# Values ahead of the probability transposes in an attention step: a fused attention and two-layer FFN kernel

## The chip, the cores and the metric

One NeuronCore of a Trainium2 chip runs the whole program. The metric is the device time of one execution in microseconds; three runs of the kernel before gave 641.52, 641.78 and 646.76 us, and their median is 641.78 us.

## The reference, cut to what matters

The inputs are q, k and v of 2 batches, 8 heads, 768 positions and 64 columns, and the weights of two feed-forward layers (512 to 2048 and back), which arrive as 64-bit floats.

```python
scores = q @ k.T / sqrt(64) + bias        # bias: minus a slope of the head times the distance
scores = where(is_global | is_local, scores, -1e9)   # 8 global keys, 96 local keys
a = softmax(scores)                       # exp(scores - max) / (sum + 1e-9)
x = (a @ v).transpose(0, 2, 1, 3).reshape(1536, 512)
x = silu(x @ w_in1) @ w_out1              # layer 1
out = hardswish(x @ w_in2) @ w_out2       # layer 2
```

## The kernel before, in words

**Units and steps.** A unit is a pair of heads and half a sequence (384 queries); there are 16 units of three tiles of 128 queries, so 48 steps in `seq` (line 442). `attention_loop(n)` (line 448) runs several stages of different steps in one turn. Turn n issues, in this order on TensorE:

- `stage_b` (line 379), the **scores** of step n: six matmuls, in pairs. Each contracts over the 64 columns of one head, so the array is used as two tiles of 64 rows (profile form `64*128`). The tile written is psS.
- `stage_c` (line 410), the **transposes of the probabilities** of step n-3 (CL = 3): four (two in a sequence's first tile) 128 by 128 transposes into psT. They use the whole array (`128*128`). The result is copied to the tile pt, by VectorE (line 419), or by ScalarE (line 421) where t is 0.
- `stage_d` (line 424), the **values** of step n-4 (LAG = 4): eight (or four) matmuls into psO, which read the pt that turn n-1 made. Each head's output has 64 columns, so the array is used as two tiles of 64 columns (`128*64`). Where t is 2, the last of a unit, ScalarE copies psO to xh (line 439), and VectorE makes the remainder xl (line 440) a turn later.
- a **piece of the feed-forward** part from `stream`, if turn n has one: 12 matmuls of `h_piece` (psH, line 510) or six of `y_piece` (psY, line 683), whole array. Pieces stand in even turns from 16; the first six places hold two pieces only (turns 16 and 22), and from turn 28 every even turn has one. Beside the turns that have transposes or values there are 14 of them, up to turn 50.
- `transposes(n)` (line 480), since APOS is 2: the **transposes of raw keys** (turns that are 2 modulo 3) or **queries** (turns that are 0 modulo 3) of a later unit into psA, three or four, whole array (lines 331 to 348). Turns that are 1 modulo 3 have none.

Turns 48 to 51 have no scores any more, only the last transposes and values with pieces. After that the program is feed-forward work alone, paced by `when` (line 210).

**Between the stages.** VectorE adds the bias and takes the extremum of the scores (line 394), ScalarE takes the exponential and its sum (line 398), VectorE the reciprocal (lines 404 and 405), GpSimd scales (line 407); then come the transposes. psS has two banks and one shared bank, psT and psA share a ring of three, psO has two.

**What sets the order.** Attention is issued under `manual_schedule` for TensorE, ScalarE and GpSimd (line 799): these run in program order. VectorE's order, and that of the loads on SyncE's queue, comes from the framework's planner, which follows program order among what it takes to be ready. Beside its own part each engine has the decoding of the 64-bit weights (lines 101 to 148), spread over the turns through `slots`.

Of the kernel before, what the change touches and what calls it, by code (L numbers as in the profile page):

```python
# [28 lines left out]
def attention_ffn_kernel(ctx, tc, q, k, v, n_global, n_local, w_in1, w_out1, w_in2, w_out2, out):  # L29
# [32 lines left out]
    def bank(tag, name):  # L62
        return psum.tile([P, 512], F32, name=name, tag=tag, bufs=ps_bufs[tag])
# [133 lines left out]
    CL = 3  # L197
# [44 lines left out]
    def loads_v(u):  # L242
        b, half, p = units[u]
        s0 = half * TB
        rv = apool.tile([P, 2, HB, D], F32, name=f"rv{u}", tag="rv")
        vp = apool.tile([P, 2, HB, D], F32, name=f"vp{u}", tag="vp")
        i0 = 1 - half
        for h in range(2):
            vh = v[b, 2 * p + h]
            nc.sync.dma_start(rv[:, h], vh[s0:s0 + TB].rearrange("(t p) d -> p t d", p=P))  # L250
            f0 = s0 - P + i0 * P
            nc.sync.dma_start(vp[:G0, h, i0:], vh[f0:f0 + (HB - i0) * P].rearrange("(t p) d -> p t d", p=P)[G:])
            nc.sync.dma_start(vp[G0:, h, i0:], vh[:G].unsqueeze(1).to_broadcast([G, HB - i0, D]))
        raw[u][3:] = rv, vp
# [44 lines left out]
    def beyond():  # L299

        fl, ng, nl = small[:, 2:5], nval[:, 0:1], nval[:, 1:2]
        nc.vector.tensor_scalar(out=fl[:, 0:1], in0=nl, scalar1=1.0, scalar2=None, op0=ALU.is_lt)
        nc.vector.tensor_scalar(out=fl[:, 1:2], in0=nl, scalar1=float(NLOC_MAX), scalar2=None, op0=ALU.is_gt)
        nc.vector.tensor_scalar(out=fl[:, 2:3], in0=ng, scalar1=float(NGLOB_MAX), scalar2=None, op0=ALU.is_gt)
        nc.vector.tensor_tensor(out=fl[:, 0:1], in0=fl[:, 0:1], in1=fl[:, 1:2], op=ALU.add)
        nc.vector.tensor_tensor(out=fl[:, 0:1], in0=fl[:, 0:1], in1=fl[:, 2:3], op=ALU.add)
        nc.vector.tensor_copy(flag, fl[:, 0:1])
# [3 lines left out]
    def biases(p):  # L311

        nbs[p] = [cpool.tile([P, 2, w], F32, name=f"{n}{p}", tag=f"{n}{p}") for n, w in (("nbB", P), ("nbA", W))]
        for nb, dist in zip(nbs[p], (distB, distA)):
            for h in range(2):
                nc.gpsimd.tensor_scalar(out=nb[:, h, :], in0=dist, scalar1=slopes[2 * p + h], scalar2=1.0, op0=ALU.mult, op1=ALU.mult)
# [59 lines left out]
    def first(u, t):  # L376
        return units[u][1] == 0 and t == 0

    def stage_b(n, u, t):
        b, half, p = units[u]  # L380
        kh, kl, qh, ql = tr[u]
        tags = ("SS", "fS", "Sf")[n % 3] if n < PRE - 1 else "SS"
        ps = [bank(tags[h], f"psS{u}_{t}_{h}") for h in range(2)]
        o = P if first(u, t) else t * SP
        for i, (a, c) in enumerate(((qh, kh), (qh, kl), (ql, kh))):
            for h in range(2):
                hs = slice(h * D, (h + 1) * D)
                nc.tensor.matmul(ps[h][:, :W], a[hs, t * P:(t + 1) * P], c[hs, o:o + W], start=i == 0, stop=i == 2)
        w, nb = (P, nbs[p][0]) if first(u, t) else (W, nbs[p][1])
        z = apool.tile([P, 2, W], F32, name=f"z{u}_{t}", tag="z", bufs=ZB)  # L390
        mn = apool.tile([P, 2], F32, name=f"mn{u}_{t}", tag="mn", bufs=3)
        sm = apool.tile([P, 2], F32, name=f"sm{u}_{t}", tag="sm", bufs=3)
        for h in range(2):
            nc.vector.tensor_tensor_reduce(  # L394
                out=z[:, h, :w], in0=ps[h][:, :w], in1=nb[:, h, :], scale=1.0, scalar=3e38,
                op0=ALU.add, op1=ALU.min, accum_out=mn[:, h:h + 1])
        for h in range(2):
            nc.scalar.activation(out=z[:, h, :w], in_=z[:, h, :w], func=AF.Exp, bias=mn[:, h:h + 1], scale=-1.0,  # L398
                                 accum_out=sm[:, h:h + 1])
        zt[u, t], smt[u, t] = z, sm  # L400

    def stage_b2(u, t):
        z, sm, w = zt[u, t], smt.pop((u, t)), P if first(u, t) else W
        nc.vector.tensor_scalar(out=sm, in0=sm, scalar1=1e-9, scalar2=None, op0=ALU.add)  # L404
        nc.vector.reciprocal(sm, sm)  # L405
        for h in range(2):
            nc.gpsimd.tensor_scalar(out=z[:, h, :w], in0=z[:, h, :w], scalar1=sm[:, h:h + 1], scalar2=1.0,  # L407
                                    op0=ALU.mult, op1=ALU.mult)

    def stage_c(u, t):  # L410
        z = zt.pop((u, t))
        n = 1 if first(u, t) else 2
        ps = bank("tr", f"psT{u}_{t}").rearrange("p (h c q) -> p h c q", h=2, c=2)
        for h in range(2):
            for c in range(n):
                nc.tensor.transpose(ps[:, h, c, :], z[:, h, c * P:(c + 1) * P], ident)
        pt = apool.tile([P, 2, 2, P], F32, name=f"pt{u}_{t}", tag="pt")
        if t:
            nc.vector.tensor_copy(pt[:, :, :n, :], ps[:, :, :n, :])
        else:  # L420
            nc.scalar.copy(pt[:, :, :n, :], ps[:, :, :n, :])
        ptt[u, t] = pt

    def stage_d(u, t):
        b, half, p = units[u]
        rk, kp, rq, rv, vp = raw[u]
        pt = ptt.pop((u, t))
        if t == 0:
            pso[0] = bank("o", f"psO{u}")
        ps = pso[0]  # L430
        n = 1 if first(u, t) else 2
        for c in range(n):
            for h in range(2):
                lhs = (rv if c == n - 1 else vp)[:, h, t, :]
                nc.tensor.matmul(ps[h * D:(h + 1) * D, t * P:(t + 1) * P], lhs, pt[:, h, c, :], start=c == 0, stop=c == n - 1)
        if t == HB - 1:
            i = 2 * b + half
            hi, lo = (x[:, p, i * TB:(i + 1) * TB] for x in (xh, xl))
            nc.scalar.copy(hi, ps[:, :TB])
            return lambda: nc.vector.tensor_tensor(out=lo, in0=ps[:, :TB], in1=hi.bitcast(F32), op=ALU.subtract)  # L440

    seq = [(u, t) for u in range(len(units)) for t in range(HB)]
    queue, late, rests, now = {}, {}, {}, [0]

    def at(n, f):
        queue.setdefault(n, []).append(f)

    def attention_loop(n):
        for f in queue.pop(n, []):
            f()  # L450
        if n < len(seq):
            u, t = seq[n]
            stage_b(n, u, t)
            if t == HB - 1 and u + 1 < NP:
                biases(u + 1)
        if n == 0:
            e, r = stage_a(1, 0)
            e()
            r()
            beyond()  # L460
        if 0 <= n - 1 < len(seq):
            stage_b2(*seq[n - 1])
        for f in rests.pop(n, []):
            f()
        if APOS == 0:
            transposes(n)
        if 0 <= n - CL < len(seq):
            stage_c(*seq[n - CL])
        if 0 <= n - LAG < len(seq):
            u, t = seq[n - LAG]  # L470
            f = stage_d(u, t)
            if f:
                at(n + 1, f)
                if u + 2 < len(units):
                    loads_v(u + 2)

        if APOS == 1:
            transposes(n)

    def transposes(n):  # L480
        for d, part in ((KOFF, 0), (QOFF, 1)):
            if (n + d) % HB == 0 and 1 <= (n + d) // HB < len(units):
                e, r = stage_a((n + d) // HB, part)
                e()
                rests.setdefault(n + 1, []).append(r)
                if part and (n + d) // HB + 2 < len(units):
                    loads((n + d) // HB + 2)
# [298 lines left out]
    def loop(n):  # L786
        now[0] = n
        attention_loop(n)
        f = todo.get(n)
        if f:  # L790
            f[0](*f[1:])
        if APOS == 2:
            transposes(n)
        for f in late.pop(n, []) + slots.pop(n, []):
            f()
# [269 lines left out]
```

## Time and profile before

| | |
|---|---|
| runs | 641.52, 641.78, 646.76 us; median 641.78 us |
| profiled execution, first to last instruction | 638.6 us |
| granted TensorE clock, mean | 0.999 |
| TensorE busy | 617.2 us, 97% of the span |
| VectorE busy | 489.9 us, 77% |
| ScalarE busy | 417.4 us, 65% |
| GpSimd busy | 161.0 us, 25% |

The profile tells the span of the profiled execution and no other time of it, so 638.6 us is the time against which rows are summed; the median of the runs is 3.2 us above it, for what lies before the first and after the last instruction recorded. A TensorE row gives the modelled end of a matmul, which overlaps the next one's start, so that the time that a group of matmuls takes on the engine is read from its start to the start of the next group, not from its duration.

### The profile page before, as it was taken

How to read it: one execution, taken by the hardware profiler on the slowest of the kernel's cores; microseconds unless marked ns; L12 is line 12 of the kernel's file. 1: busy time of each engine (PE TensorE's matmuls, PEld its weight loads, DVE VectorE, ACT ScalarE, POOL GpSimd, SP SyncE). 2: the span in 40 equal slices, each digit the busy share in tenths (PEclk: the TensorE clock that was granted, in tenths of full speed). 3: DMA queues.
4: the chain of work that ended last, by engine and by line, in shares of the span. 5: the costliest groups of instructions: out<-in, count | busy, mean ns of one | idle time of the engine just before them, and what ended most of it. 6: DMA issues, size and time to landing. Idle time of an engine off the chain costs nothing.

```text
span 638.6 us, 9729 instructions
## 1 busy us (share of the span) xinstructions
PE 617.2 (97%) x3214; PEld 498.9 (78%) x3214; DVE 489.9 (77%) x1107; ACT 417.4 (65%) x887; POOL 161.0 (25%) x233
## 2 busy tenths in 40 slices
PE   5889999999999999999999998999999999999996
PEld 3667777789888788888888887887788888888885
DVE  5899889953578796767675679988979696969453
ACT  4787877765557576666666676765766666666760
POOL 2776666561111111111212120011111111111110
PEclk9999999999999999999999999999999999999999
DMA  6555645349577667777776793186576868686544
GB/s 174 136 139 136 149 112 137 99 150 204 103 162 166 144 146 176 161 180 166 181 163 134 164 198 100 66 247 150 132 173 165 182 157 181 157 176 162 100 102 166
DMA packets 81625, 97.31 MB, mean 152 GB/s; under 512 B 55456, under 2 KB 55456, under 8 KB 81312
## 3 DMA queue, kind: packets, MB, share of 16 engines
q0 software_dynamic: 12576, 45.09, 37.7%
q1 hardware_dynamic: 68992, 51.53, 26.8%
q8 instruction: 27, 0.44, 0.3%
q14 instruction: 30, 0.25, 0.1%
HBM read 46.27 MB, written 3.15 MB: 77 GB/s over the span
## 4 chain that ended last, share of the span: by engine, by line
PE 35%; issue 25%; POOL 5%; DVE 2%; DMA 2%; ACT 1%; POOLq 0%; ACTq 0%; SPq 0%; DVEq 0%
PE psY L683 19%; PE psH L510 9%; POOL y L712 5%; PE psP_b L591 3%; PE psP_c L591 2%; PE psP_a L591 2%; DMA y<-st 1%; DMA raw<-in_moe_w_in_dram 1%; ACT st L708 0%; DVE g L541 0%; DVE da L1027 0%; DVE wol L148 0%; DVE dc L134 0%; DVE u L608 0%; ACT da L103 0%
## 5 line engine op out<-in xcount | busy, mean ns | idle before, releaser
L712 POOL DMA_DIRECT2D y<-st x78 | 66.9, 857 | 362.4 <-ACT st L708 357.2
L708 ACT COPY st<-psY 128x512 f32<-128x512 f32 x156 | 91.3, 586 | 51.6 <-PE psY L683 47.5
L510 PE MATMUL psH<-xh,wih 128*128 128x512 f32 (+1 forms) x216 | 83.2, 385 | 1.7 <-DVE g L541 1.7
L510 PE MATMUL psH<-xl,wih 128*128 128x512 f32 (+1 forms) x216 | 82.5, 382 | 0.0
L510 PE MATMUL psH<-xh,wil 128*128 128x512 f32 (+1 forms) x216 | 82.4, 382 | 0.0
L683 PE MATMUL psY<-gh,woh 128*128 128x512 f32 (+1 forms) x160 | 61.4, 384 | 0.0
L683 PE MATMUL psY<-gh,wol 128*128 128x512 f32 (+1 forms) x160 | 60.6, 378 | 0.0
L683 PE MATMUL psY<-gl,woh 128*128 128x512 f32 (+1 forms) x160 | 60.5, 378 | 0.0
L398 ACT ACTIVATE z<-z,mn 128x256 f32<-128x256 f32 (+1 forms) x96 | 46.5, 486 | 21.1 <-DVE mn L394 15.6
L407 POOL TENSOR_SCALAR z<-z,sm 128x256 f32<-128x256 f32 (+1 forms) x96 | 48.2, 514 | 43.9 <-DVE sm L405 18.4
L683 PE MATMUL psY<-woh,gl 128*128 128x512 f32 x144 | 56.1, 390 | 0.1
L683 PE MATMUL psY<-woh,gh 128*128 128x512 f32 x144 | 56.1, 390 | 0.1
L683 PE MATMUL psY<-wol,gh 128*128 128x512 f32 x144 | 56.0, 389 | 0.0
L510 PEld LDWEIGHTS psH<-xh,wih 128*128 128x128 f32 x216 | 40.5, 188 | 10.6 <-DVE g L541 2.1
L103 ACT ACTIVATE da<-raw 128x512 f32<-128x512 f32 x64 | 42.9, 670 | 5.9 <-DMA raw<-in_moe_w_in_dram 5.5
L510 PEld LDWEIGHTS psH<-xl,wih 128*128 128x128 f32 x216 | 40.5, 188 | 7.5 <-DVE xl L620 0.4
L510 PEld LDWEIGHTS psH<-xh,wil 128*128 128x128 f32 x216 | 40.5, 188 | 7.1
L1027 DVE SCALAR_TENSOR_TENSOR da<-raw,da 128x512 int32<-128x512 int32 x64 | 44.3, 693 | 1.2 <-DVE sm L404 0.2
L608 DVE TENSOR_TENSOR u<-psP_c,u 128x512 f32<-128x512 f32 x22 | 15.1, 688 | 34.5 <-ACT u L602 34.5
L532 ACT ACTIVATE a<-psH 128x512 f32<-128x512 f32 (+1 forms) x24 | 14.2, 590 | 40.4 <-PE psH L510 40.3
L551 DVE SCALAR_TENSOR_TENSOR gl<-a,gh 128x512 fp32r<-128x512 f32 (+1 forms) x34 | 23.2, 682 | 21.9 <-ACT gh L545 21.6
L1015 DVE TENSOR_SCALAR da<-da 128x512 f32<-128x512 f32 x64 | 28.3, 442 | 14.7 <-ACT da L103 14.7
(185 smaller groups left out, 1565.2 us busy)
## 6 DMA issues: line engine op xcount, KB each, us to landing
y<-st POOLq DMA_DIRECT2D x78, 512.0 KB, 4.8
raw<-in_moe_w_in_dram SPq DMA_DIRECT2D x32, 512.0 KB, 4.1
raw<-in_moe_w_out_dram SPq DMA_DIRECT2D x32, 512.0 KB, 3.3
rk<-in_k_dram SPq DMA_DIRECT2D x32, 96.0 KB, 2.5
rq<-in_q_dram SPq DMA_DIRECT2D x32, 96.0 KB, 2.9
rv<-in_v_dram SPq DMA_DIRECT2D x32, 96.0 KB, 2.6
out_dram<-y SPq DMA_DIRECT2D x12, 256.0 KB, 2.0
xf<-xh SPq DMA_DIRECT2D x2, 1024.0 KB, 6.7
```

The lines of the kernel that those rows point to most:

```text
L103: nc.scalar.activation(out=t["a"], in_=raws[n][:, :, 1].bitcast(F32), func=AF.Abs)
L398: nc.scalar.activation(out=z[:, h, :w], in_=z[:, h, :w], func=AF.Exp, bias=mn[:, h:h + 1], scale=-1.0, accum_out=sm[:, h:h + 1])
L407: nc.gpsimd.tensor_scalar(out=z[:, h, :w], in0=z[:, h, :w], scalar1=sm[:, h:h + 1], scalar2=1.0, op0=ALU.mult, op1=ALU.mult)
L510: nc.tensor.matmul(ps, a[:, kt, js], x[:, kt, n0:n1], start=n == 0, stop=n == 3 * KT - 1)
L551: nc.vector.scalar_tensor_tensor(out=gl[:, j, :], in0=t["a"], scalar=2.0, in1=gh[:, j, :].bitcast(F32), op0=ALU.mult, op1=ALU.subtract)
L591: nc.tensor.matmul(ps, a[:, 2 * k + q, f * P:(f + 1) * P], x, start=p in (1, 5) and n == 0, stop=n == 5, skip_group_check=True)
L608: nc.vector.tensor_tensor(out=u, in0=st["c"], in1=u, op=ALU.add)
L683: nc.tensor.matmul(ps[:, :rhs.shape[1]], lhs, rhs, start=n == 0, stop=n == 3 * FC - 1)
L708: nc.scalar.copy(st[:, m % 2, :], part)
L712: late.setdefault(n, []).append(lambda: nc.gpsimd.dma_start(y, st, accum_op=ALU.add))
L1015: nc.vector.tensor_scalar(out=a, in0=a, scalar1=as_float(897 << 20), scalar2=as_float((1151 << 20) - 1), op0=ALU.max, op1=ALU.min)
L1027: nc.vector.scalar_tensor_tensor(out=ai, in0=w1, scalar=-0x40000000, in1=ai, op0=ALU.bitwise_and, op1=ALU.bitwise_or)
```

## The change

In `attention_loop` the call of `stage_d` for step n-4 moves ahead of the call of `stage_c` for step n-3. TensorE's order in a turn becomes scores, values, transposes of the probabilities, piece, raw transposes. Along with `stage_d` move the copy of psO to xh on ScalarE (where t is 2) and the loads of the values of unit u+2, which are issued behind it. In turns that are 0 modulo 3 both `stage_c` (t = 0) and `stage_d` (t = 2) have work on ScalarE, so there the copy to xh now stands ahead of the copy to pt.

```diff
         if APOS == 0:
             transposes(n)
-        if 0 <= n - CL < len(seq):
-            stage_c(*seq[n - CL])
         if 0 <= n - LAG < len(seq):
             u, t = seq[n - LAG]
             f = stage_d(u, t)
@@
                 at(n + 1, f)
                 if u + 2 < len(units):
                     loads_v(u + 2)
+        if 0 <= n - CL < len(seq):
+            stage_c(*seq[n - CL])
```

## Rows read from the trace of the kernel before

**Rows 1.** The page, busy time, share of the span and instructions of each engine

```profile
PE 617.2 (97%) x3214; PEld 498.9 (78%) x3214; DVE 489.9 (77%) x1107; ACT 417.4 (65%) x887; POOL 161.0 (25%) x233
```

**Rows 2.** Windows of 40 us: length, busy us and instructions by engine, clock, DMA

```profile
20.00:60.00 40.00, 35.89 (x324) 25.41 (x323) 37.47 (x142) 31.19 (x104) 29.32 (x49) 1.00 0.62 152
60.00:100.00 40.00, 38.66 (x322) 28.92 (x322) 36.48 (x135) 29.89 (x99) 25.93 (x40) 1.00 0.53 133
100.00:140.00 40.00, 39.85 (x345) 30.52 (x341) 33.33 (x119) 29.04 (x94) 27.09 (x40) 1.00 0.39 97
```

**Rows 3.** Waits of TensorE: us in total, times, longest us

```profile
PE psO L435 <- DVE pt L419: 2.9, 3, 1.1
```

**Rows 4.** Timeline, TensorE, 103 to 108: start us, us, operation, [idle before]

```profile
103.48 0.44 PE L683 MATMUL psY<-gh,woh 128*128 128x384 f32 x1
103.76 0.34 PE L683 MATMUL psY<-gl,woh 128*128 128x384 f32 x1
103.94 0.34 PE L683 MATMUL psY<-gh,wol 128*128 128x384 f32 x1
...
105.60 0.66 PE L416 MATMUL psT<-ident,z 128*128 128x128 f32 x4
106.18 0.44 PE L435 MATMUL psO<-pt,rv 128*64 128x128 f32 x4
106.55 0.39 PE L388 MATMUL psS<-kh,qh 64*128 64x256 f32 x2
...
107.11 0.66 PE L416 MATMUL psT<-ident,z 128*128 128x128 f32 x4
107.70 0.44 PE L435 MATMUL psO<-pt,vp 128*64 128x128 f32 x4
```

**Rows 5.** Timeline, TensorE, 109 to 113

```profile
109.44 0.49 PE L331 MATMUL psA<-ident,rk 128*128 128x128 f32 x3
109.77 0.27 PE L346 MATMUL psA<-ident,kp 128*128 128x128 f32 x1
...
111.70 0.55 PE L331 MATMUL psA<-ident,rq 128*128 128x128 f32 x3
112.17 0.39 PE L388 MATMUL psS<-kh,qh 64*128 64x256 f32 x2
...
112.73 0.66 PE L416 MATMUL psT<-ident,z 128*128 128x128 f32 x4
```

**Rows 6.** Timeline, TensorE's weight loads, 103 to 104

```profile
103.48 0.19 PEld L683 LDWEIGHTS psY<-gh,woh 128*128 128x128 f32 x1 [0.17 <-issue]
103.59 0.19 PEld L683 LDWEIGHTS psY<-gl,woh 128*128 128x128 f32 x1
```

**Rows 7.** Timeline, TensorE, 136 to 138, a turn without scores

```profile
136.54 0.60 PE L416 MATMUL psT<-ident,z 128*128 128x128 f32 x4
137.07 0.44 PE L435 MATMUL psO<-pt,vp 128*64 128x128 f32 x4
...
137.66 0.66 PE L416 MATMUL psT<-ident,z 128*128 128x128 f32 x4
```

**Rows 8.** Timeline, VectorE, the copies at 106.86 and 138.35

```profile
106.86 0.68 DVE L419 COPY pt<-psT 128x512 f32<-128x512 f32 x1
...
138.35 0.69 DVE L419 COPY pt<-psT 128x512 f32<-128x512 f32 x1 [0.48 <-PE psT L416]
```

**Rows 9.** Timeline, ScalarE, 112 to 113

```profile
112.31 0.56 ACT L421 COPY pt<-psT 128x512 f32<-128x512 f32 x1
112.77 0.48 ACT L439 CAST xh<-psO 128x384 fp32r<-128x384 f32 x1
113.14 0.50 ACT L337 ACTIVATE qh<-psA 128x384 fp32r<-128x384 f32 x1
```

**Rows 10.** Timeline, TensorE, 27 to 30, an early turn

```profile
27.89 0.66 PE L416 MATMUL psT<-ident,z 128*128 128x128 f32 x4
29.63 0.51 PE L435 MATMUL psO<-pt,vp 128*64 128x128 f32 x4 [1.08 <-DVE pt L419]
```

## The prediction, made before the kernel ran

> **What bounds the kernel now.** I read the page's busy times first: TensorE 97% of the span [rows 1], so the time is TensorE's as long as nothing makes it wait. Then the windows: from 100 to 140 us it is busy for 39.85 of 40 us and VectorE for 33.33, while from 20 to 60 us VectorE has 37.47 and TensorE 35.89 [rows 2]. The reader should see two regimes: early VectorE is the tighter engine, later TensorE is. The waits say the same: TensorE stood before the values three times for the copy of the probabilities by VectorE, 2.9 us in all [rows 3], all early, as at 29.63 [rows 10]. Last I read TensorE's timeline turn by turn, from start to start. The change touches only the 48 turns of attention and the four behind them; what it gains or loses there moves the whole rest, which is TensorE work end to end.
>
> **What is saved: changes of the array's tiling.** Three transposes in a row, from 109.44 to 109.77, take 0.33 us, so 0.11 each within one tiling [rows 5]. A group of four between groups of other tilings takes 0.59 (107.11 to 107.70) [rows 4], 0.15 over 4 x 0.11; one of three takes 0.47 (111.70 to 112.17) [rows 5], 0.14 over. So entering and leaving the whole-array tiling costs about 0.15 us. After a piece, in the same tiling, four transposes take 0.53 (136.54 to 137.07), after values 0.59 [rows 7, 4]: entering is 0.06 of it, leaving 0.09. A piece that follows values has its first two matmuls 0.28 apart and the next two 0.18 [rows 4]: 0.10 more for entering.
> - Turns with raw transposes and no piece: the two groups become one of seven or eight, and one 0.15 goes. By the turn rules there are 27 turns with raw transposes from turn 3 on, 5 of them with a piece and one with no values yet; 21 x 0.15 = 3.2 us.
> - Turns with a piece, 14: leaving (0.09) and the piece's entering (0.10) go; 14 x 0.19 = 2.7 us.
> - Turns with neither keep three changes.
> Together 5.9 us. Scores then values is a neighbourhood that no row shows. Every kind that is shown costs alike, so I take 0.15 for it as for scores then transposes; the bounds are nothing (45 turns x 0.15 = 6.8 us less) and twice (6.8 us more).
>
> The Trainium skill (TensorEngine Tiling (Array Packing), Key Properties) says that a change of tiling mode drains the engine; by that rule scores to values would not be free, and no run here shows it yet. A rule of the Trainium skill speaks against part of the gain: TensorE: Matmul & The Clock Gate, Part 3, The mechanism, has weight loads overlap a running matmul only where the row group differs, so a whole-array piece could hide no load behind whole-array transposes, and only leaving would be saved. The trace disagrees: the piece's second load starts at 103.59, 0.11 after its first matmul at 103.48 and well before the next at 103.76 [rows 6, 4].
>
> **What is added: a shorter way from a copy to its reader.** The values of a step read the pt that was copied from the transposes of the turn before. Before, those transposes were followed by the values of another step, the piece, the raw transposes, the scores and the next transposes. Now the other values stand ahead of them and the next transposes behind the reader: the reader wants to start about where the next psT group started before. Its cost is how much later than that its copy ends, rounded up a little for the release.
> - Turns with a piece: six or twelve matmuls 0.17 to 0.18 apart, 1 to 2 us, lie between [rows 4]; nothing to pay. This piece is the cover; without it the next two cases apply.
> - Odd turns with neither piece nor raw transposes (19, 25, 31, 37, 43): the copy at 106.86 ends at 107.54 [rows 8], the next psT group began at 107.11 [rows 4], so 0.43, about 0.5 us each with the release: 2.5 us. The bounds are nothing and that.
> - Early turns of that kind, three waits of rows 3: VectorE is late anyway. Before, the transposes (0.59) ran inside the wait, from 27.89 while the values waited until 29.63 [rows 10]; now they start after the values, and what they fed comes later. Bounds: nothing, if the later copies have time in hand, and 0.59 each; VectorE, the tight engine there, reads these transposes next, so I take a value near the upper one, 0.5 x 3 = 1.5 us.
> - The copy of a unit's first tile, on ScalarE, turns that are 0 modulo 3. The cast of psO to xh now goes ahead of it: the cast's turn on ScalarE is 0.37 (112.77 to 113.14); the copy ended at 112.87, 0.14 after the next psT group began at 112.73 [rows 9, 5]. So 0.51 at most, 0.55 with the release. Of 16 such turns four have a piece, one has no values yet, and one I leave out for a delay before it: ten, 5.5 us at most, and nothing at least, if the cast, ready 0.6 us earlier than it was, gets through in a gap of ScalarE. No row is nearer to one end than to the other; I take half, 2.8 us. Queued behind cast and copy on ScalarE are the queries' evacuation and the next exponentials, which scores two turns on need; they move by no more than the 0.37 swapped.
> - The tail: in turns 48 and 50 nothing stands between the transposes of the odd turn before and the values that read them. The psT group at 137.66 has its copy from 138.35 to 139.04 [rows 7, 8], 1.38 after its start; 0.59 of that is its own run, so 0.79 us of waiting, twice: 1.7 us with the release.
> - SyncE: the loads of values for unit u+2 are issued a little earlier in program order, into a ring of two that the same values free; nothing waits for it. GpSimd has nothing that moves. VectorE's work is the same, but the planner may set it in another order, which I can't price; it is in the range.
>
> **The sum**: -5.9 + 2.5 + 1.5 + 2.8 + 1.7 = +2.6 us, on a span of 638.6 us; with the 3.2 us around it unchanged that is 641.8 + 2.6 = **644.4 us**, slower by 0.4%. A difference under 1% is about what a measurement of this kernel can't tell from no change.
>
> **The rivals.**
> - *Nearly even* (forecast), chance 0.50: savings and waits as above. Its own range is 641 to 648: the waits other than the tail's at a third of their upper bounds, 9.8 / 3 + 1.7 - 5.9 = -0.9, or in full, 9.8 + 1.7 - 5.9 = +5.6.
> - *The evacuations keep up*, 0.22: TensorE comes later to its transposes only by what it did before them, the engines that copy catch up during the first wait, and the later ones vanish. For it: VectorE has 6.7 us free from 100 to 140 [rows 2]. Against it: the copy at 106.86 was in VectorE's order behind work on the same turn's scores. Only the tail and two of the three early waits stay: -5.9 + 1.7 + 1.0 = -3.2, so 638.6 us; with half the price for scores to values 635.2.
> - *ScalarE's order decides* (slower), 0.20: the cast waits for the last values of a unit, those wait for a VectorE copy, and the unit's next copy stands behind the cast although its transposes could run. Its place is the ten exposed turns, its price the 0.55 plus the values' own time, for which the transposes' 0.59 stands (107.11 to 107.70) [rows 4]: 11.4 us in place of 2.8, so 641.8 + 2.6 + 8.6 = 653 us if all ten pay, 649 if two thirds do. It decides when the cast's start, rather than the second exponential, releases the copy. For it: the cast follows the copy at once now (112.31, 112.77) [rows 9], so ScalarE has no gap there; against it: where values come earlier the cast may be ready before the exponentials end.
> - *It only moves the limit*, 0.06: VectorE is the limit wherever TensorE gains, and the planner's order absorbs the rest; 641 to 643 us.
> - *Only draining is saved*, 0.02: 35 turns x 0.09 = 3.2 us instead of 5.9, so 647.1 us. It follows from the load not being hidden, which rows 6 speak against; the Trainium skill's rule on row groups (TensorE: Matmul & The Clock Gate, Part 3) would give it.
>
> **How the numbers follow.** The point is the likeliest case's, 644.4. The range goes from 637.5, inside the second case, to 651, most of the third; I leave out about 0.1 at each end, where scores to values costs nothing or double. Faster by over 1% means under 635.4: the second case with a cheap change from scores to values, 0.05. Slower by over 1% means above 648.2: most of the third case and the upper edge of the first, 0.22. Within 1%: 0.73. Most of the middle is on the slow side of even, with the saving's total of 5.9 us, 0.9%, as the wall on the fast side.
>
> **What would show it.** A joined group of transposes at 0.11 each across psT and psA, and a first gap of 0.18 in a piece, show the saving; a longer time from the first scores to the first values than it was to the first transposes corrects the price of that neighbourhood. Waits of the values for the copies by VectorE and ScalarE in the list of waits, about 8 us more than the 2.9 now and mostly in turns without a piece, show the cost; the cast ahead of the copy on ScalarE with the copy's end half a microsecond later shows its part. I am wrong if that list hardly grows, or if TensorE's stretch up to the last values gets shorter by over 5 us, or longer by over 8.

## The result and the profile after

The changed kernel takes 645.69 us (median of 20 runs, 644.3 to 649.67), the kernel before 641.84 us beside it (20 runs); the ratio is 1.0055, 95% interval 1.004 to 1.0071. That is 3.9 us slower by the medians and 3.5 by the ratio, inside 1%. The forecast was 644.4 us, +2.6.

The page of the changed kernel, busy time by engine, answers to [rows 1]:

```profile
PE 614.7 (95%) x3214; PEld 500.7 (78%) x3214; DVE 488.3 (76%) x1107; ACT 418.1 (65%) x887; POOL 160.8 (25%) x233
```

TensorE has the same 3214 matmuls and is busy for 2.5 us less, yet the profiled span is 644.1 us instead of 638.6: it now stands idle. The 5.5 us between the two spans are more than the change, though. In every run whose span is on record the time is 1.7 to 1.9 us above the span, so of the 3.2 us named ahead of the prediction only about 1.8 lie outside the recorded instructions: the profiled execution of the kernel before, some 640.4 us long, was as fast as the fastest of the 20 runs (640.45), while that of the changed kernel is a typical one (its runs' median span is 643.9 us).

The windows of 40 us say where, beside [rows 2]:

```profile
20.00:60.00 40.00, 34.11 (x293) 25.48 (x291) 34.72 (x134) 28.36 (x96) 28.68 (x48) 0.96 0.59 143
60.00:100.00 40.00, 36.06 (x329) 28.07 (x331) 35.02 (x138) 31.20 (x103) 24.53 (x40) 1.00 0.57 133
100.00:140.00 40.00, 36.60 (x323) 29.33 (x323) 34.01 (x122) 29.51 (x96) 24.82 (x37) 1.00 0.43 105
```

From 100 to 140 us, where TensorE was busy for 39.85 us, it is now for 36.60. VectorE's window is hardly fuller (34.01 us instead of 33.33): no other engine became the bound, TensorE waits. The list of its waits (us in total, times, longest) names what for, beside [rows 3]:

```profile
PE psO L435 <- ACT pt L421: 7.7, 11, 1.4
...
PE psO L435 <- DVE pt L419: 6.3, 10, 1.7
```

14.0 us in 21 waits where there were 2.9 in three, all of them of the values for the two copies. The first window also shows a granted clock of 0.96; it comes back below.

The saving, and the neighbourhood that no row of before had, stand in TensorE's timeline of turns 41 and 42:

```profile
121.46 0.66 PE L416 MATMUL psT<-ident,z 128*128 128x128 f32 x4
121.96 0.49 PE L331 MATMUL psA<-ident,rk 128*128 128x128 f32 x3
122.28 0.27 PE L346 MATMUL psA<-ident,kp 128*128 128x128 f32 x1
122.49 0.39 PE L388 MATMUL psS<-kh,qh 64*128 64x256 f32 x2
...
123.04 0.44 PE L435 MATMUL psO<-pt,vp 128*64 128x128 f32 x4
...
123.62 0.66 PE L416 MATMUL psT<-ident,z 128*128 128x128 f32 x4
124.04 0.42 PE L683 MATMUL psY<-gh,woh 128*128 128x384 f32 x1
124.29 0.33 PE L683 MATMUL psY<-gl,woh 128*128 128x384 f32 x1
```

Eight joined transposes go from 121.46 to 122.49, 1.03 us: 8 x 0.11 and one 0.15, not two. From the transposes' start to the piece's second matmul it is 0.67 (123.62 to 124.29) where the separate groups took 0.59 + 0.28 [rows 4]: 0.20 less. Scores to values takes 0.55 (122.49 to 123.04), and scores to transposes took 0.56 in [rows 4] (106.55 to 107.11): the unknown price is the common one.

The cost in an exposed turn that is 0 modulo 3, on ScalarE, beside [rows 9], and on TensorE:

```profile
115.48 0.50 ACT L398 ACTIVATE z<-z,mn 128x256 f32<-128x256 f32 x1
115.88 0.19 ACT L398 ACTIVATION_READ_ACCUMULATOR z<-z,mn 128x1 f32 x1
115.98 0.45 ACT L439 CAST xh<-psO 128x384 fp32r<-128x384 f32 x1
116.34 0.58 ACT L421 COPY pt<-psT 128x512 f32<-128x512 f32 x1
```

```profile
116.97 0.51 PE L435 MATMUL psO<-pt,vp 128*64 128x128 f32 x4 [0.89 <-ACT pt L421]
```

ScalarE runs through without a gap: exponentials, cast, copy, the copy's end at 116.92, the values 0.05 behind it after 0.89 us of idling. And the tail, beside [rows 7, 8]:

```profile
138.26 0.66 PE L416 MATMUL psT<-ident,z 128*128 128x128 f32 x4
139.70 0.44 PE L435 MATMUL psO<-pt,vp 128*64 128x128 f32 x4 [0.78 <-DVE pt L419]
```

From transposes to values 1.44 us, with nothing between but the copy: 0.85 over the 0.59 of before, as forecast.

### The profile page after: what moved, and what is told of

Read it like the earlier page. It is cut to its first block, busy times and chain, and to the rows that moved or that the text cites. A ratio compares the mean times of both kernels' runs of the same rounds, so it can differ in the third digit from the quotient of the medians.

```text
span 644.1 us, 9743 instructions
## 1 busy us (share of the span) xinstructions
PE 614.7 (95%) x3214; PEld 500.7 (78%) x3214; DVE 488.3 (76%) x1107; ACT 418.1 (65%) x887; POOL 160.8 (25%) x233
## 4 chain that ended last, share of the span: by engine, by line
PE 35%; issue 25%; POOL 5%; DVE 2%; DMA 2%; ACT 1%; POOLq 0%; ACTq 0%; SPq 0%; DVEq 0%
PE psY L683 19%; PE psH L510 8%; POOL y L712 5%; PE psP_b L591 3%; PE psP_c L591 2%; PE psP_a L591 2%; DMA y<-st 1%; DMA raw<-in_moe_w_in_dram 1%; ACT st L708 0%; DVE g L541 0%; DVE da L1027 0%; DVE wol L148 0%; DVE u L608 0%; DVE dc L134 0%; ACT da L103 0%
## 5 line engine op out<-in xcount | busy, mean ns | idle before, releaser
L683 PE MATMUL psY<-gl,woh 128*128 128x512 f32 (+1 forms) x160 | 60.5, 378 | 0.0
L551 DVE SCALAR_TENSOR_TENSOR gl<-a,gh 128x512 fp32r<-128x512 f32 (+1 forms) x34 | 23.2, 682 | 21.7 <-ACT gh L545 21.4
```

The costliest lines, as they stand in the source:

```text
L551: nc.vector.scalar_tensor_tensor(out=gl[:, j, :], in0=t["a"], scalar=2.0, in1=gh[:, j, :].bitcast(F32), op0=ALU.mult, op1=ALU.subtract)
L683: nc.tensor.matmul(ps[:, :rhs.shape[1]], lhs, rhs, start=n == 0, stop=n == 3 * FC - 1)
```

## The experiments

Seven other kernels, the changed kernel once more, and second profiles of two. The runs stand in three sets, each on one chip with the kernel before beside it, whose median differed between the sets (642.23, 644.3 and 642.54 us), so the ratios are what compares.

**The changed kernel again** (no edit).

> The changed kernel once more, for the runs beside it and for a second profile. Theory (late copies): about 3.9 us above the kernel before, waits of the values for the two copies near 14 us in all, and nearly all of them in turns behind a turn without a piece. Rival (the first profile caught something odd: its granted clock was 0.96 from 20 to 60 us, and its span stands 5.5 us above that of before, where the runs differ by 3.9): the long wait near 30 us and the half clock behind it are not there a second time, and the span is near 642.5 us.

645.44 us against 642.23, ratio 1.0049 (1.0029 to 1.0069). The time repeats; the span, 642.6 us, came out as the rival said, but this profiled execution (644.35 us) is the fastest of the twelve. The waits:

```profile
PE psO L435 <- ACT pt L421: 7.8, 11, 1.4
...
PE psO L435 <- DVE pt L419: 3.4, 8, 0.8
```

A further 2.3 us in front of the values the list puts down to loads; with them it is 13.5 us. In both profiles every one of these waits stands in a turn behind a turn without a piece, and none behind a piece: the cover is what decides. In the first profile the values idled 1.75 us near 31 us and the granted clock fell behind it, which these windows of 2 us show:

```profile
30.00:32.00 2.00, 0.95 (x8) 0.79 (x8) 2.00 (x9) 0.63 (x4) 1.39 (x5) 0.72 0.54 123
32.00:34.00 2.00, 2.00 (x11) 1.57 (x8) 1.21 (x4) 0.53 (x3) 2.00 (x4) 0.50 0.25 62
```

0.50 is the lower of the two levels, 1.2 GHz. In the second profile the same wait was 0.95 us and the windows are granted 1.00; that turn took 3.3 us there and 5.4 in the first profile. So some 2 us of the first profile are a longer wait (0.8) and a stretch of half clock that such a wait may bring on and need not; they are no part of every run.

**The copy ahead of the cast.** TensorE's order stays changed, ScalarE's goes back.

```diff
-            nc.scalar.copy(hi, ps[:, :TB])
...
+            return (lambda: nc.scalar.copy(hi, ps[:, :TB]),
...
             f = stage_d(u, t)
...
         if 0 <= n - CL < len(seq):
             stage_c(*seq[n - CL])
+        if f:
+            f[0]()
+            at(n + 1, f[1])
...
```

> TensorE as in the changed kernel, values ahead of transposes, but on ScalarE the copy of the transposes stands ahead of the cast of psO again. Theory (the cast takes 0.37 us ahead of the copy in each of the ten or eleven exposed turns): waits for ScalarE's copy fall from 7.7 us by about 4 us, and the time from 645.7 to some 642 us. Rival (the copy is released by the exponentials ahead of it on ScalarE, and the cast runs in a gap): those waits stay within 1 us of 7.7, and the time within 1 us of 645.7.

```profile
PE psO L435 <- DVE pt L419: 8.0, 10, 1.8
...
PE psO L435 <- ACT pt L421: 3.8, 8, 1.0
```

The waits for ScalarE fell by 3.9 us, as the theory had it, but the time only to 644.54, ratio 1.0033 (1.0014 to 1.0052): 1 us, not 4, and even that is not clear of noise, since the interval overlaps that of the changed kernel. Of what ScalarE gave back 1.7 us were waited for again at VectorE's copies in the turns behind, 8.0 us in all. This profile too has the long wait near 31 us with half clock behind it, so against the first profile the waits' sum fell from 14.0 to 11.8. ScalarE's order is a real part of the waits; what it is worth in time is less than they suggest.

**The values last.**

```diff
         if APOS == 2:
             transposes(n)
+        if 0 <= n - LAG < len(seq):
+            u, t = seq[n - LAG]
+            f = stage_d(u, t)
...
```

> Scores, transposes of the probabilities, piece, raw transposes, then the values of step n-4: also three changes of tiling in a turn with whole-array work instead of four, but a turn's whole work between a copy and its reader. Theory (savings near 6 us are real, the waits ate them): waits of the values for copies under 3 us, and a time near 636 to 637.5 us, faster than both. Rival (the changes of tiling are worth little, since each engine's share of the work limits the turn): 640.5 to 643 us.

640.70 us, ratio 0.9955 (0.9931 to 0.9979): faster than both, by 2.9 us of the ratio (1.5 by the medians), not by the 5 to 6 expected; 640.70 lies in the rival's range. The waits for copies are gone (0.4 us, once), and in TensorE's timeline the joined groups are there as in the changed kernel, seven transposes in 0.92 us, so the rival's reason does not hold for them:

```profile
110.99 0.66 PE L416 MATMUL psT<-ident,z 128*128 128x128 f32 x4
111.49 0.49 PE L331 MATMUL psA<-ident,rq 128*128 128x128 f32 x3
111.91 0.44 PE L435 MATMUL psO<-pt,vp 128*64 128x128 f32 x4
```

From the scores of turn 20 to those of turn 47, at full clock in both kernels, it needs 72.3 us where the kernel before needs 74.4, in the first profiles and in the second ones below: 2.1 us are saved there, and the waits of the scores for VectorE's extremum grew from 0.4 us to 1.5. The early turns lose: between the scores of turns 16 and 20 it needs 11.7 us where the kernel before needs 10.6 (48.7 to 60.5, and 47.3 to 57.9), and in this profile the full clock came only at 29:

```profile
25.91 0.58 PE L388 MATMUL psS<-kh,qh 64*128 64x256 f32 x2
...
29.11 0.39 PE L388 MATMUL psS<-kh,qh 64*128 64x256 f32 x2
```

The same pair of score matmuls shows 0.58 us at the lower level and 0.39 at the higher. A **second profile** of this kernel and of the one before:

> A second look at the kernel with the values last. In its first profile TensorE was granted full clock only from 29.0 us, in that of the kernel before from 20.2. Theory (the saving is there and the clock's start took part of it): if the full clock comes earlier, the last values start near 135 to 137 us, against 140.1 before. Rival: the last values stay near 139.5 us with an early clock as well.

> A second look at the kernel before. Theory (the start of the full clock differs from run to run, whatever the kernel): it comes some us away from 20.2, and the last values move by about half of what it moves. Rival (the order decides when the clock is granted): within 1 us of 20.2.

The kernel before: full clock from 21.5 us, 1.3 later than at first, and last values at 140.8, 0.7 later: half of it, as its theory had it. With the values last: full clock from 21.4 to 24.8, half to 31.6, last values at 140.8 too. (In its first profile they start at 140.0; the 139.5 of the expectation are the values of turn 50.) So this profile could not give what the theory asked for, an early clock, and its test is open: both profiles have 7 to 9 us more of half clock than those of the kernel before, and still reach the last values as early. Across all profiles the start of full clock came between 20.2 and 29.0 us.

**The values a turn later** (in the changed order).

```diff
-    LAG = CL + 1
+    LAG = CL + 2
```

> The changed order with LAG = CL + 2: the values of step n-5 stand ahead of the transposes, so a copy has a turn more; pieces start a turn later, and one more turn without scores stands at the end. Theory: waits of the values for copies under 3 us, time 636.5 to 639 us, a little above the kernel with the values last for the added turn. Rival (scores followed by values, whose tilings differ in rows and columns, are slow in themselves): waits gone and still 642 us or more.

643.35 us, ratio 1.0009 (0.9987 to 1.0031): the waits for copies vanish from the list, the changed order's loss with them, but the gain does not appear. New waits took their place, of the scores for VectorE's extremum (2.7 us where the kernel before has 0.4) and of the values for their own loads:

```profile
53.67 0.47 PE L435 MATMUL psO<-pt,vp 128*64 128x128 f32 x1 [2.73 <-DMA vp<-in_v_dram]
...
54.71 1.12 PE L416 MATMUL psT<-ident,z 128*128 128x128 f32 x4
```

The ring of value tiles has two places, and values that read a turn later free them a turn later. Behind the 2.73 us four transposes take 1.12 us instead of 0.66: half clock again, from 52.8 to 59.6. It is no accident of this profile: eight of the twelve runs have a mean granted clock of 0.994 or less, and none of the 35 runs of the kernel before beside them has under 0.995. The rival's numbers came out, waits gone and over 642 us, but not for its reason: scores to values was not slow.

**The two halves of the change.** Values ahead of the transposes only where the turn before had a piece, and only where it had none:

```diff
+        covered = todo.get(n - 1) is not None
+        early = covered            # the other kernel: not covered
+        if not early and 0 <= n - CL < len(seq):
+            stage_c(*seq[n - CL])
         if 0 <= n - LAG < len(seq):
...
-        if 0 <= n - CL < len(seq):
+        if early and 0 <= n - CL < len(seq):
             stage_c(*seq[n - CL])
```

> Values ahead of the transposes only in turns whose turn before had a piece (17, 23, 29, 31 and every odd turn to 51), the order of the kernel before in all others. Theory (the new order costs only where the way from copy to reader is short): no new waits of the values for copies, seven turns with raw transposes save 0.15 us each, so 1 us less than the kernel before, near 641.2 us. Rival (values straight behind scores, or the cast ahead of the copy, cost by themselves): slower than before by about 1.5 us, since 18 of the 48 turns have the new order.

643.22 us against 644.3, ratio 0.9999 (0.9973 to 1.0026). No loss shows, but the interval reaches 1.7 us either way, so the times exclude neither the saving of 1 us nor the rival's loss of 1.5. The trace says more: turns 17, 23, 29, 35, 39 and 41 are 0.14 to 0.16 us shorter each, so straight behind scores the values cost nothing by themselves (the seventh, 33, saved 0.03). The waits for VectorE's copy grew from 2.9 to 3.5 us, and those for ScalarE's from none to 0.4.

> The other half: values ahead only in turns whose turn before had no piece. Theory: up to turn 28, where pieces are rare, the waits stay as in the changed kernel, near 9 us with those of the kernel before in them; later the transposes of the turn before run 0.59 us earlier than in the changed kernel, so its waits shrink to less than half. 4.9 us are saved, so 643.5 to 645 us. Rival (as above): proportional to the turns, 30 of 48, some 644.5 us too, but with the later waits as in the changed kernel, 6 us behind turn 28.

644.53 us, ratio 1.0015 (0.9991 to 1.004), so +1 us with an interval that takes in zero, a little under the 1.7 to 3.2 expected. The waits:

```profile
PE psO L435 <- ACT pt L421: 6.0, 11, 1.3
PE psO L435 <- DVE pt L419: 4.2, 10, 0.7
```

10.2 us, and 1.0 more that the list puts down to loads; behind 90 us they are 3.2 against 5.3 in the changed kernel, less of a fall than the half expected, more than the rival's none. By the point values the halves' costs don't add up to the whole's 3.5, though their intervals leave room for it. A reason that the waits behind 90 us bear out in part: a turn in the old order makes its transposes 0.59 us earlier, which the next turn's values profit from.

**From turn 21 on.** The old order to turn 20, then once the values last, once the changed order (`if n >= 21` around the same edits).

> The order of the kernel before up to turn 20, then the values last in every turn. Theory (with the values last the early turns lose what the later ones save, 1.2 us between turns 16 and 20, and to a clock granted late): ten turns x 0.15 plus thirteen x 0.19 are saved, 4.0 us, less some 0.8 us of new waits, so 638.6 to 639.2 us, and full clock from 20 to 22 us as in the kernel before. Rival (the clock's start has nothing to do with the order): a start of full clock spread as before, and no better than the values last throughout, 640.7 us.

641.38 us, ratio 0.9981 (0.9964 to 0.9997). That is a gain of 1.2 us (0.2 to 2.3), where the theory asked for 2.6 to 3.2, and no more than the values last throughout, so my theory of the early turns fell. Its profile has the order of the kernel before in the first turns and full clock only from 25.9 us, against 20.2 and 21.5: there the clock's start moved with no change of order ahead of it.

> The order of the kernel before up to turn 20, the changed order from turn 21 on. Theory (in the changed kernel's second profile turns 16 to 20 lost 1.7 us, turns 20 to 47 about 0.5, the tail 1.2): 1.5 to 2 us above the kernel before, 643.5 us, with 3 us of waits for the copies of ScalarE and 4 for those of VectorE, the tail's among them. Rival (the early turns cost nothing, as VectorE was late there anyway): 3.5 to 4 us above, like the changed kernel.

644.94 us, ratio 1.0035 (1.002 to 1.005), +2.2 us, nearer to the theory's 1.5 to 2 than to the rival's 3.5 to 4, which its interval (1.3 to 3.2) leaves out, with 4.3 us of waits for ScalarE and 5.9 for VectorE (2.9 of them those of the kernel before), more than the 3 and 4 expected. So by the point values the later turns and the tail carry some two thirds of the loss.

## Why the prediction was right

**The mechanism** was right: the forecast said that the saving is real, that a shorter way from a copy to its reader eats it, and that a piece in between is the cover. The joined groups, the list of waits and the turns in which they stand show all three, and with the values last the joined groups stay, the waits go and the kernel is faster.

**The savings** were right to the hundredth where a turn waits for nothing: between the two second profiles turns with raw transposes and no piece became 0.14 to 0.16 us shorter, turns with both (30, 36 and 42) 0.20, turns with neither (31, 37 and 43) changed by 0.01. A wait takes more than the idle time listed: turns 32 and 38, which also have both, became 0.38 and 0.55 longer, so with 0.20 saved the wait cost 0.58 and 0.75 for 0.42 and 0.45 of idle. The rule of the Trainium skill (TensorE: Matmul & The Clock Gate, Part 3, The mechanism) by which only the leaving, 0.09, would be saved, does not fit these rows: from the transposes' start to the piece's second matmul 0.20 went, not 0.09. The Trainium skill's other rule (TensorEngine Tiling (Array Packing), Key Properties), that a change of mode drains, agrees with scores to values at 0.55 us, the price of every other change.

**The tail**: 1.7 us forecast, 0.78 us of idling twice measured, as the row of 139.70 shows.

**Odd turns without cover**: 2.5 us forecast; five waits of 0.23 to 0.45 us of idle, in turns 20, 26, 32, 38 and 44, make 1.6.

**ScalarE's copy** was the term mis-sized: 2.8 us taken, 5.5 as the upper bound, 7.7 measured. I had put the copy's lateness at 0.51 from one turn, 0.37 of it the cast's. The cast's part was right at its upper bound: without it ahead 3.9 us of waits went. The other 3.8 are the copy's own lateness, taken as 0.14 in a turn and up to 1.0 without the cast ahead: exponentials of the turn, cast and copy run on ScalarE without a gap, and in front of the longest wait, 1.4, the exponentials themselves stand behind a decoding of weights (line 103). The third case's condition was not met: in every exposed turn the cast follows the exponentials at once and waits for no values, and its price of 11.4 was not reached.

**The early turns**: 1.5 us forecast, and none of it shows. The three waits are 2.2 us in place of 2.9, and against the second profile of the kernel before, whose clock starts alike, the changed kernel's second profile is level at turn 16 and loses after it.

| scores of turn, start in us | 16 | 20 | 47 | last values | span |
|---|---|---|---|---|---|
| before, second profile | 48.0 | 58.6 | 133.0 | 140.8 | 640.1 |
| changed, second profile | 47.9 | 60.2 | 135.1 | 144.1 | 642.6 |

The balance of these two: waits for copies +10.6 us (13.5 less 2.9); savings -5.9, as counted in the forecast; other waits that shrank or went -2.1 (the transposes no longer wait, 0.9 and 0.5 us; a piece of layer 2 0.5 less; the first keys' load 0.2 less). That is +2.6, and the spans differ by 2.5. The forecast's sum had the same terms with smaller waits, 8.5, and no such relief: two errors of some 2 us that cancelled. Within the waits ScalarE's copies were taken 5 us too low, the early turns 2 and the odd turns 0.9 too high. So it was luck that the sum agrees to 0.1 us with these two profiles.

Of the rivals, keeping up was wrong: from 100 to 140 us VectorE had 34.01 of 40 us busy in the changed kernel and still made the values wait, since what counts is the time from one set of transposes to its copy's end, not VectorE's share. What the time of 3.5 to 3.9 has over the profiles' 2.5 stays open. Half clock behind long waits, as in the first profile, is not all of it: a stretch of 3.4 us at half clock takes 0.0026 off a run's mean granted clock, so a run at 0.998 or more had none. Ten of the 20 runs of the changed kernel had 0.998 or more, with a median span of 643.7 us, 3.7 above the 640.0 that the median of the kernel before gives. How late full clock first came is not in that mean (it reads 1.00 for the first 20 us, where four transposes take 1.12 us), and may be part of it.

One cause is untested. The planner set VectorE in another order too: in the trace of the changed kernel some remainders xl and some decoding stand at other places among the copies. No run holds that order fixed, so what it adds to or takes off the waits is not shown.

## What to carry to other kernels

A reorder that saves changes of the array's tiling is worth counting, here in turns times 0.15 to 0.2 us, and in turns that wait for nothing it came out just so; but look at what the order had put between a producer's evacuation and its reader. Put the moved group where it joins its like and lengthens that way: with the values last the joined groups stayed and the waits for copies went, 0.45% faster than the kernel before, where the values first were 0.55% slower. And of a wait taken away on one engine's copy a part, here 1.7 us of 3.9, is waited for again at the next one's.

## What the runs showed of the hardware

Scores on 64-row tiles followed by values on 64-column tiles cost what the change from scores to the whole array costs: 0.55 us from the first score's start to the first value's, against 0.56 to the first transpose's. The time at which TensorE was first granted full clock differed from 20.2 to 29.0 us between profiles, and among those with the same first turns from 20.2 to 25.9; waits of 1.75 us (changed kernel), 2.73 (values a turn later) and, with the values last, 2.09 and 1.57 had stretches of 3.4 or 6.8 us at half clock begin in them or within 1.1 us behind them, while those of 0.95 and 1.08 had none, and neither had one of 1.69 at 386 us in the kernel before: the length of a wait alone does not decide it. Four transposes took 1.12 us at half clock and 0.66 at full, so that by estimate such a stretch costs some 1.4 to 2.8 us, not much less than this whole change.
